# A mixture-of-experts stage behind a gated recurrence: from all experts on all tokens to tokens sorted by expert, gathered and scattered by indirect DMA

## The chip, the cores and the metric

One Trainium2 chip, one of its cores, one launch. Times are device microseconds of that core; a result is the median of its runs. The engines are TensorE (PE, its weight loads as PEld), VectorE (DVE), ScalarE (ACT), GpSimd (POOL) and SyncE (SP, which here only issues DMAs).

## What is computed

The kernel has two parts. The first is a gated linear recurrence in 768 steps for 4 batches of 8 heads of width 48, with a complex decay: `S = a * S + k v^T`, `y_t = q_t S_re`. Its output, put side by side by heads, is a matrix x of 3072 tokens by 384. The second part is a mixture of experts on x. For each token, 8 logits are x times a gate matrix plus a bias that the token's modality picks; the largest logit picks the expert, and its softmax probability is the weight of the result:

```python
logits = x @ w_gate + modality_bias[modality_id]
e_idx = np.argmax(logits, axis=1)
for e in range(E):
    mask = e_idx == e
    h = np.maximum(x[mask] @ w1[e], 0.0)
    out[mask] = gate_w[mask, None] * (h @ w2[e])
```

w1 is 8 x 384 x 1024 and w2 is 8 x 1024 x 384, in float32. Only one expert of eight is needed for a token.

## The kernel before

The kernel is written in a tile framework: tiles come from pools with a number of buffers, and the framework puts in the semaphores. It orders each engine's instructions by program order and by when they can start, so an engine's queue may differ from the text: a tile whose space is taken from closed pools waits for the tiles that held it.

**Attention, 6 chunks of 128 steps.** For each of 32 (batch, head) pairs a helper, `load_t` (L159 to L166), loads a 128x48 piece through SP into `raw` (two buffers), transposes it on PE and copies it on VectorE; it runs for a_re, a_im, q and k. VectorE then normalises the decay and forms its running products over the chunk in seven doubling steps (L194 to L211). A loop over the 32 heads (L242 to L282) multiplies on PE with VectorE copies between; `y_sb` (L261, two buffers) holds a head's 128x48 result, which PE transposes, VectorE copies to `yT_sb` (L265), and SP stores to `x_attn` in HBM with tokens along the row (L267). Sixteen VectorE instructions (L288 to L303) then carry the state to the next chunk. `gstack.close()` gives the space of these tiles back.

**Experts, `moe_bf16` (L18).** x is loaded transposed, as one 4.7 MB DMA (L32), and cast to bf16 (L34). For 24 tiles of 128 tokens, three f32 matmuls with an 8-wide moving side make the logits (L47), and small VectorE and ScalarE instructions make a table `sc_all` that has the gate weight in the column of the picked expert and zero elsewhere (L71). Then every expert runs on every token: for each expert its float32 weights are loaded through SP (L81, L85) and cast on VectorE (L82, L86), two buffers each; for each of 6 blocks of 512 tokens and each of 8 slices of F there are three matmuls 512 wide (L93), a relu on VectorE from PSUM to bf16 (L95), and four matmuls 384 wide that sum into four PSUM banks (L97). At the block's end VectorE multiplies by the table's column and adds to `out_acc` (L100). The last expert's results are stored tile by tile (L102). The lines after the early `return` in the main function never run.

Of the kernel before, what the change touches and what calls it, by code (L numbers as in the profile page):

```python
# [17 lines left out]
def moe_bf16(nc, ctx, tc, cpool, ppool, x_dram, moe_modality_id, moe_w_gate, moe_modality_bias, moe_w1, moe_w2, out):  # L18
    Dt, N = x_dram.shape
# [3 lines left out]
    nDC = Dt // 128  # L23
    nT = 128
    nTiles = N // nT
    nF = F // 128

    mp = ctx.enter_context(tc.tile_pool(name="mp", bufs=2))
    mbig = ctx.enter_context(tc.tile_pool(name="mbig", bufs=1))

    xT = mbig.tile([128, nDC, N], F32, name="xT")
    nc.sync.dma_start(out=xT[:], in_=x_dram.rearrange("(dc p) n -> p dc n", p=128))  # L32
    xTb = mbig.tile([128, nDC, N], BF16, name="xTb")
    nc.vector.tensor_copy(xTb[:], xT[:])  # L34

    mb_raw = cpool.tile([1, nM * E], F32, name="mb_raw")
# [367 lines left out]
```

## Time and profile before

| | us |
|---|---|
| median of 3 runs | 4122.12 |
| lowest and highest run | 4119.45 and 4122.41 |
| span of the profiled execution, first to last instruction | 4111.5 |
| median less span | 10.6 |
| attention stage, to its last state update | 3525.4 |
| load of x, gate, experts | 586.1 |

The time of the profiled execution is known by its span alone; it is set against the median of the runs. In the rows below, PE and PEld are two rows of one engine, "x" is a count, a releaser is what an engine waited for last, and "SPq" is the queue of DMA issues on SP. Matmul ends are modelled, so the start-to-start distance of matmuls tells more than their duration.

### The profile page before, as it was taken

The page shows a single profiled execution, that of the slowest core. Times are in us where ns is not written, and L with a number is a line of the kernel's source. Part 1 is how long each engine was busy: PE and PEld are TensorE (multiplying, and loading weights), DVE is VectorE, ACT ScalarE, POOL GpSimd, SP SyncE. Part 2 cuts the span into 40 slices and gives each one's busy share as a digit, 9 for nine tenths or more (in the row PEclk, how much of TensorE's full clock was granted, in tenths as well). Part 3 has the DMA queues.
Part 4 walks back from the last instruction along what each step waited for, and adds up shares of the span by engine and source line. Part 5 has one row for each costly group of instructions (what it writes and reads, how often), then busy time and mean ns, then how long its engine had stood idle before and what let it go on. Part 6 is the DMA issues. An engine that isn't in the chain of part 4 may idle for free.

```text
span 4111.5 us, 21704 instructions
## 1 busy us (share of the span) xinstructions
PE 1639.4 (40%) x6816; PEld 959.5 (23%) x6864; DVE 2761.7 (67%) x3610; ACT 29.2 (1%) x32; POOL 57.5 (1%) x199
## 2 busy tenths in 40 slices
PE   2002751013740015720027610137400157599999
PEld 0000540002520004500005400025200035444444
DVE  4997246986248984259972469872489842877676
ACT  0000000000000000000000000000000000000000
POOL 0000000000000000000000000000000000000000
PEclk9999999999999999999999999999999999999999
DMA  1000000000010000010000000000100000401001
GB/s 25 0 2 13 5 16 11 0 9 8 5 22 5 0 12 6 5 25 0 0 15 5 15 13 0 7 9 5 21 6 0 12 5 5 170 31 62 31 1 47
DMA packets 167188, 64.41 MB, mean 16 GB/s; under 512 B 143138, under 2 KB 163618, under 8 KB 166690
## 3 DMA queue, kind: packets, MB, share of 16 engines
q1 hardware_dynamic: 167074, 63.02, 6.1%
q8 instruction: 56, 0.92, 0.1%
q14 instruction: 58, 0.48, 0.0%
HBM read 53.51 MB, written 9.44 MB: 15 GB/s over the span
## 4 chain that ended last, share of the span: by engine, by line
DVE 51%; PE 33%; DMA 10%; issue 3%; POOL 1%; ACT 1%; DVEq 0%; POOLq 0%; SPq 0%; ACTq 0%
PE z_ps L97 6%; PE hT_ps L93 5%; DVE qc L203 4%; DVE kc L204 4%; DVE kc L201 4%; DVE qc L200 4%; DVE cr L185 4%; DVE qc L231 4%; DMA raw<-in_a_im_dram 3%; PE Wt_ps L252 3%; DMA raw<-in_q_dram 3%; PE y_ps L258 3%; PE tp L165 3%; PE y_ps L259 3%; DMA raw<-in_a_re_dram 3%
## 5 line engine op out<-in xcount | busy, mean ns | idle before, releaser
L165 PE MATMUL tp<-ident,raw 128*48 128x128 f32 x768 | 286.6, 384 | 2052.1 <-DVE qc L166 1315.0
L165 PEld LDWEIGHTS tp<-ident,raw 128*48 128x48 f32 x768 | 88.3, 116 | 2249.1 <-DVE qc L166 1432.1
L95 DVE TENSOR_SCALAR hT<-hT_ps 128x512 bf16<-128x512 f32 x384 | 254.2, 689 | 134.4 <-PE hT_ps L93 119.3
L262 DVE COPY y_sb<-y_ps 128x48 f32<-128x48 f32 x192 | 39.9, 208 | 409.5 <-PE y_ps L260 409.5
L97 PE MATMUL z_ps<-w2e,hT 128*128 128x384 bf16 x1536 | 283.8, 328 | 9.0 <-DVE hT L95 7.0
L93 PE MATMUL hT_ps<-xTb,w1e 128*128 128x512 bf16 x1104 | 271.2, 380 | 2.8 <-issue 0.2
L252 PE MATMUL Wt_ps<-are,cr 48*128 48x128 f32 x384 | 152.3, 499 | 107.0 <-DVE cr L235 107.0
L258 PE MATMUL y_ps<-vc,Wt 128*128 128x48 f32 x384 | 127.0, 431 | 161.8 <-POOL Wt L256 161.8
L255 DVE COPY Wt<-Wt_ps 128x128 f32<-128x128 f32 x192 | 55.9, 291 | 190.5 <-PE Wt_ps L253 190.5
L97 PEld LDWEIGHTS <-hT 128*128 128x128 bf16 x1536 | 122.3, 97 | 177.7 <-DVE hT L95 127.1
L185 DVE RECIPROCAL cr<-cr 48x4096 f32<-48x4096 f32 x6 | 154.5, 25745 | 0.2
L231 DVE RECIPROCAL qc<-qc 48x4096 f32<-48x4096 f32 x6 | 154.4, 25734 | 0.0
L258 PEld LDWEIGHTS y_ps<-vc,Wt 128*128 128x128 f32 x384 | 96.2, 311 | 218.3 <-POOL Wt L256 218.3
L166 DVE COPY aim<-tp 48x128 f32<-48x128 f32 x192 | 52.5, 282 | 133.5 <-PE tp L165 133.3
L93 PEld LDWEIGHTS <-w1e 128*128 128x128 bf16 x1152 | 113.1, 98 | 118.5 <-issue 1.3
L166 DVE COPY are<-tp 48x128 f32<-48x128 f32 x192 | 52.3, 281 | 115.0 <-PE tp L165 114.5
L259 PE MATMUL y_ps<-S0rA,are 48*128 48x48 f32 x384 | 126.7, 428 | 0.0
L252 PEld LDWEIGHTS Wt_ps<-are,cr 48*128 48x128 f32 x384 | 95.9, 308 | 125.6 <-DVE cr L235 108.7
L253 PE MATMUL Wt_ps<-aim,ci 48*128 48x128 f32 x384 | 121.1, 417 | 0.0
L260 PE MATMUL y_ps<-S0iA,kc 48*128 48x48 f32 x384 | 119.7, 410 | 0.0
L266 DVE COPY yT_sb<-yT_ps 48x128 f32<-48x128 f32 x192 | 54.3, 283 | 96.4 <-PE yT_ps L264 96.4
L166 DVE COPY qc<-tp 48x128 f32<-48x128 f32 x192 | 50.1, 280 | 101.7 <-PE tp L165 101.4
(101 smaller groups left out, 2984.6 us busy)
## 6 DMA issues: line engine op xcount, KB each, us to landing
w1f<-in_moe_w_dram SPq DMA_DIRECT2D x8, 1536.0 KB, 6.5
w2f<-in_moe_w_dram SPq DMA_DIRECT2D x8, 1536.0 KB, 8.2
vc<-in_v_dram SPq DMA_DIRECT2D x24, 192.0 KB, 3.7
raw<-in_a_re_dram SPq DMA_DIRECT2D x192, 24.0 KB, 1.7
raw<-in_a_im_dram SPq DMA_DIRECT2D x192, 24.0 KB, 1.6
raw<-in_q_dram SPq DMA_DIRECT2D x192, 24.0 KB, 1.7
raw<-in_k_dram SPq DMA_DIRECT2D x192, 24.0 KB, 1.7
x_attn<-yT_sb SPq DMA_DIRECT2D x192, 24.0 KB, 1.4
```

The source lines that it names most:

```text
L93: nc.tensor.matmul(hT_ps[:], w1e[:, dc, fc * 128:(fc + 1) * 128], xTb[:, dc, t0:t0 + TTK], start=(dc == 0), stop=(dc == nDC - 1))
L95: nc.vector.tensor_relu(hT[:], hT_ps[:])
L97: nc.tensor.matmul(z_ps[z][:], hT[:, z * nT:(z + 1) * nT], w2e[:, fc, :], start=(fc == 0), stop=(fc == nF - 1))
L165: nc.tensor.transpose(tp[:], raw[:], ident[:L, :L])
L185: nc.vector.reciprocal(tmp[:], tmp[:])
L200: nc.vector.tensor_tensor(tA[:, :, :, :n_], a_hi, a_lo, Alu.mult)
L201: nc.vector.tensor_tensor(tB[:, :, :, :n_], b_hi, b_lo, Alu.mult)
L203: nc.vector.tensor_tensor(tA[:, :, :, :n_], a_hi, b_lo, Alu.mult)
L231: nc.vector.reciprocal(qf[:], qf[:])
L252: nc.tensor.matmul(Wt_ps[:], Kr[:], Qr[:], start=True, stop=False)
L258: nc.tensor.matmul(y_ps[:], Wt[:], vb, start=True, stop=False)
L259: nc.tensor.matmul(y_ps[:], Qr[:], S0r[bh][:], start=False, stop=False)
```

## The change

The expert stage is written anew as `moe_sorted`. Attention also stores `y_sb`, with tokens as rows, to a second HBM tensor `x_rows`. All 8 experts' weights are loaded once through POOL's queue by DMAs that cast to bf16, into two tiles that hold all experts. Logits are computed with the gate as the stationary side and transposed back. Each token gets a slot number from its expert: matmuls with triangular and all-one matrices count tokens before it, and scans make the experts' offsets, each rounded up to 128. One-hot products of slot and token invert the permutation into `idg` (a token for each slot), `ids` (the same, with 8192 or so, out of bounds, for an empty slot) and the gate weight of each slot. Then 31 slots of 128 tokens run: an indirect DMA gathers the slot's rows of x with a cast to bf16, the slot's expert number is loaded into a PE register, PE transposes the rows, multiplies with that expert's weights by a register-addressed slice, VectorE and ScalarE share the relu, ScalarE scales, and an indirect DMA scatters the rows to the output, leaving out-of-bounds rows out. The main function's dead code goes, and the attention stage's PSUM pool is closed with it.

Core of the diff:

```diff
@@ moe_bf16 -> moe_sorted @@
-def moe_bf16(nc, ctx, tc, cpool, ppool, x_dram, moe_modality_id, moe_w_gate, moe_modality_bias, moe_w1, moe_w2, out):
...
-    for nt in range(nTiles):
-        n0 = nt * nT
-        lg_ps = ppool.tile([nT, E], F32, name="lg_ps", tag="r", bufs=4)
-        for dc in range(nDC):
-            nc.tensor.matmul(lg_ps[:], xT[:, dc, n0:n0 + nT], wg[:, dc, :], start=(dc == 0), stop=(dc == nDC - 1))
...
-        w1e = mp.tile([128, nDC, F], BF16, name="w1e")
-        w1f = mp.tile([128, nDC, F], F32, name="w1f")
-        nc.sync.dma_start(out=w1f[:], in_=moe_w1[e].rearrange("(dc p) f -> p dc f", p=128))
-        nc.vector.tensor_copy(w1e[:], w1f[:])
-        w2e = mp.tile([128, nF, Dt], BF16, name="w2e")
-        w2f = mp.tile([128, nF, Dt], F32, name="w2f")
-        nc.sync.dma_start(out=w2f[:], in_=moe_w2[e].rearrange("(fc p) d -> p fc d", p=128))
-        nc.vector.tensor_copy(w2e[:], w2f[:])
-        for tk in range(nTK):
-            t0 = tk * TTK
-            z_ps = [ppool.tile([nT, Dt], F32, name=f"z_ps{i}", tag=f"z{i}", bufs=1) for i in range(TTK // nT)]
-            for fc in range(nF):
-                hT_ps = ppool.tile([128, TTK], F32, name="hT_ps", tag="r", bufs=4)
-                for dc in range(nDC):
-                    nc.tensor.matmul(hT_ps[:], w1e[:, dc, fc * 128:(fc + 1) * 128], xTb[:, dc, t0:t0 + TTK], start=(dc == 0), stop=(dc == nDC - 1))
-                hT = mp.tile([128, TTK], BF16, name="hT")
-                nc.vector.tensor_relu(hT[:], hT_ps[:])
-                for z in range(TTK // nT):
-                    nc.tensor.matmul(z_ps[z][:], hT[:, z * nT:(z + 1) * nT], w2e[:, fc, :], start=(fc == 0), stop=(fc == nF - 1))
-            for z in range(TTK // nT):
-                nt = tk * (TTK // nT) + z
-                nc.vector.scalar_tensor_tensor(out_acc[:, nt, :], z_ps[z][:], sc_all[:, nt, e:e + 1], out_acc[:, nt, :], Alu.mult, Alu.add)
-    for nt in range(nTiles):
-        nc.sync.dma_start(out=out[nt * nT:(nt + 1) * nT, :], in_=out_acc[:, nt, :])
+def moe_sorted(nc, ctx, tc, cpool, ident, x_t_dram, x_rows_dram, moe_modality_id, moe_w_gate, moe_modality_bias, moe_w1, moe_w2, out):
...
+    mp = ctx.enter_context(tc.tile_pool(name="mp", bufs=1))
+    fp = ctx.enter_context(tc.tile_pool(name="fp", bufs=3))
+    pp = ctx.enter_context(tc.psum_pool(name="pp", bufs=1))
+    w1s = mp.tile([128, E, KD, F], BF16, name="w1s")
+    w2s = mp.tile([128, E, NF, Dt], BF16, name="w2s")
+    xT = mp.tile([128, KD, N], F32, name="xT", tag="xT")
+    wg = mp.tile([128, KD, E], F32, name="wg")
+    mb = mp.tile([128, nM, E], F32, name="mb")
+    mid = mp.tile([128, NT, 2], I32, name="mid")
+    nc.sync.dma_start(out=wg[:], in_=moe_w_gate.rearrange("(k p) e -> p k e", p=128))
+    nc.sync.dma_start(out=mb.rearrange("p m e -> p (m e)"), in_=moe_modality_bias.rearrange("m e -> (m e)")[None, :].broadcast_to([128, nM * E]))
+    nc.sync.dma_start(out=mid[:], in_=moe_modality_id.bitcast(I32).rearrange("(t p two) -> p t two", p=128, two=2))
+    for k in range(KD):
+        nc.sync.dma_start(out=xT[:, k, :], in_=x_t_dram[k * 128:(k + 1) * 128, :])
     for e in range(E):
+        nc.gpsimd.dma_start(out=w1s[:, e], in_=moe_w1[e].rearrange("(k p) f -> p k f", p=128))
+        nc.gpsimd.dma_start(out=w2s[:, e], in_=moe_w2[e].rearrange("(c p) d -> p c d", p=128))
...
+    io128 = mp.tile([128, 128], F32, name="io128")
+    nc.gpsimd.iota(io128[:], pattern=[[1, 128]], base=0, channel_multiplier=0, allow_small_or_imprecise_dtypes=True)
+    idp1 = mp.tile([128, NT], F32, name="idp1")
+    nc.gpsimd.iota(idp1[:], pattern=[[128, NT]], base=1, channel_multiplier=1, allow_small_or_imprecise_dtypes=True)
+    pref = mp.tile([128, E], F32, name="pref")
+    nc.gpsimd.iota(pref[:], pattern=[[-1, E]], base=E, channel_multiplier=0, allow_small_or_imprecise_dtypes=True)
...
+    lg_ps = pp.tile([128, NT, E], F32, name="lg_ps")
+    for j in range(N // 512):
+        ps = pp.tile([E, 512], F32, name="lgT_ps", tag="r", bufs=2)
+        lgT = fp.tile([E, 512], F32, name="lgT", bufs=2)
+        sl = slice(j * 512, (j + 1) * 512)
+        for k in range(KD):
+            nc.tensor.matmul(ps[:], wg[:, k, :], xT[:, k, sl], start=(k == 0), stop=(k == KD - 1))
+        nc.scalar.copy(lgT[:], ps[:])
+        for i in range(4):
+            nc.tensor.transpose(lg_ps[:, 4 * j + i, :], lgT[:, i * 128:(i + 1) * 128], ident[:E, :E])
...
+    cand = mp.tile([128, NT, E], F32, name="cand")
+    nc.vector.scalar_tensor_tensor(cand[:], sh[:], 0.0, pref[:, None, :].broadcast_to([128, NT, E]), Alu.is_ge, Alu.mult)
+    best = mp.tile([128, NT], F32, name="best")
+    nc.vector.tensor_reduce(best[:], cand[:], axis=AX.X, op=Alu.max)
+    oneh = mp.tile([128, NT, E], BF16, name="oneh")
+    nc.vector.tensor_tensor(oneh[:], cand[:], bc(best, E), Alu.is_equal)
+    rank_ps = pp.tile([128, NT, E], F32, name="rank_ps", tag="rk")
+    nc.tensor.matmul(rank_ps.rearrange("p t e -> p (t e)"), trib[:], oneh.rearrange("p t e -> p (t e)"), start=True, stop=True)
+    cnt_ps = pp.tile([128, NT, E], F32, name="cnt_ps", tag="ct")
+    nc.tensor.matmul(cnt_ps.rearrange("p t e -> p (t e)"), onesb[:], oneh.rearrange("p t e -> p (t e)"), start=True, stop=True)
+    cnt = mp.tile([128, E, NT], F32, name="cnt")
+    nc.vector.tensor_copy(cnt[:], cnt_ps.rearrange("p t e -> p e t"))
+    inc = mp.tile([128, E, NT], F32, name="inc")
+    nc.vector.tensor_tensor_scan(inc.rearrange("p e t -> p (e t)"), seg0.rearrange("p e t -> p (e t)"), cnt.rearrange("p e t -> p (e t)"), 0.0, Alu.mult, Alu.add)
...
+    texp = mp.tile([128, H32], I32, name="texp")
+    nc.vector.tensor_scalar(texp[:], texp_f[:], float(E - 1), None, Alu.min)
...
+    onlo = mp.tile([128, NT, 128], F32, name="onlo", tag="xT")
+    nc.vector.tensor_tensor(onlo[:], io128[:, None, :].broadcast_to([128, NT, 128]), bc(lo, 128), Alu.is_equal)
...
+    inv_ps = pp.tile([128, 2, H32], F32, name="inv_ps", tag="ct")
+    for t in range(NT):
+        nc.tensor.matmul(inv_ps.rearrange("p a h -> p (a h)"), onlo[:, t, :], load[:, t].rearrange("p a h -> p (a h)"), start=(t == 0), stop=(t == NT - 1))
...
+    idg = mp.tile([128, H32], U32, name="idg")
+    nc.vector.tensor_scalar(idg[:], inv[:, 0, :], -1.0, 0.0, Alu.add, Alu.max)
+    empty = mp.tile([128, H32], F32, name="empty")
+    nc.vector.tensor_scalar(empty[:], inv[:, 0, :], 0.0, 8192.0, Alu.is_equal, Alu.mult)
+    ids = mp.tile([128, H32], U32, name="ids")
+    nc.vector.scalar_tensor_tensor(ids[:], inv[:, 0, :], -1.0, empty[:], Alu.add, Alu.add)
+    for i in range(NS):
+        xg = fp.tile([128, Dt], BF16, name="xg", bufs=4)
+        nc.gpsimd.indirect_dma_start(out=xg[:], out_offset=None, in_=x_rows_dram, in_offset=bass.IndirectOffsetOnAxis(ap=idg[:, i:i + 1], axis=0))
+        te = nc.values_load(texp[0:1, i:i + 1], engines=[ET.PE], min_val=0, max_val=E - 1, skip_runtime_bounds_check_because="a count of at most E, cut at E - 1")
+        xg_ps = pp.tile([128, KD, 128], BF16, name="xg_ps", tag="rk")
+        for k in range(KD):
+            nc.tensor.transpose(xg_ps[:, k, :], xg[:, k * 128:(k + 1) * 128], identb[:])
+        xgT = fp.tile([128, KD, 128], BF16, name="xgT")
+        nc.vector.tensor_copy(xgT[:], xg_ps[:])
+        hT = fp.tile([128, NF, 128], BF16, name="hT", bufs=2)
+        for g in range(2):
+            h_ps = pp.tile([128, NF // 2, 128], F32, name="h_ps", tag="r", bufs=2)
+            for f in range(NF // 2):
+                ff = g * (NF // 2) + f
+                for k in range(KD):
+                    nc.tensor.matmul(h_ps[:, f, :], w1s[:, bass.ds(te, 1), k, ff * 128:(ff + 1) * 128], xgT[:, k, :], start=(k == 0), stop=(k == KD - 1))
+            gs = slice(g * (NF // 2), (g + 1) * (NF // 2))
+            if g == 0:
+                nc.vector.tensor_relu(hT[:, gs], h_ps[:])
+            else:
+                nc.scalar.activation(hT[:, gs], h_ps[:], Act.Relu)
+        y_ps = pp.tile([128, Dt], F32, name="y_ps", tag="y", bufs=2)
+        for f in range(NF):
+            nc.tensor.matmul(y_ps[:], hT[:, f, :], w2s[:, bass.ds(te, 1), f, :], start=(f == 0), stop=(f == NF - 1))
+        y_sb = fp.tile([128, Dt], F32, name="y_sb")
+        nc.scalar.activation(y_sb[:], y_ps[:], Act.Copy, scale=inv[:, 1, i:i + 1])
+        nc.gpsimd.indirect_dma_start(out=out, out_offset=bass.IndirectOffsetOnAxis(ap=ids[:, i:i + 1], axis=0), in_=y_sb[:], in_offset=None, bounds_check=N - 1, oob_is_err=False)
...
     x_dram = nc.dram_tensor("x_attn", (Dt, N), F32, kind="Internal").ap()
+    x_rows = nc.dram_tensor("x_rows", (N, Dt), F32, kind="Internal").ap()
 
     cpool = ctx.enter_context(tc.tile_pool(name="c", bufs=1))
-    ppool = ctx.enter_context(tc.psum_pool(name="ps", bufs=2))
     gstack = ExitStack()
+    ppool = gstack.enter_context(tc.psum_pool(name="ps", bufs=2))
...
             y_sb = pool.tile([L, D], F32, name="y_sb")
             nc.vector.tensor_copy(y_sb[:], y_ps[:])
+            nc.sync.dma_start(out=x_rows[b * S + t0:b * S + t0 + L, h * D:(h + 1) * D], in_=y_sb[:])
             yT_ps = ppool.tile([D, L], F32, name="yT_ps", tag="r", bufs=4)
             nc.tensor.transpose(yT_ps[:], y_sb[:], ident[:L, :L])
             yT_sb = pool.tile([D, L], F32, name="yT_sb")
...
     gstack.close()
-    if True:
-        moe_bf16(nc, ctx, tc, cpool, ppool, x_dram, moe_modality_id, moe_w_gate, moe_modality_bias, moe_w1, moe_w2, out)
-        return
...
+    moe_sorted(nc, ctx, tc, cpool, ident, x_dram, x_rows, moe_modality_id, moe_w_gate, moe_modality_bias, moe_w1, moe_w2, out)
```

## Rows read from the trace of the kernel before

**Rows 1.** Page, part 1: busy us, share of the span, instructions, by engine

```profile
PE 1639.4 (40%) x6816; PEld 959.5 (23%) x6864; DVE 2761.7 (67%) x3610; ACT 29.2 (1%) x32; POOL 57.5 (1%) x199
```

**Rows 2.** Windows by stage: length, busy us of each engine, granted clock, DMA share, GB/s

```profile
0.00:3504.45 3504.45, 1087.80 (x4032) 693.24 (x4032) 2316.68 (x2716) 22.98 (x7) 57.47 (x199) 1.00 0.04 8
3504.45:3525.40 20.95, 0.00 (x0) 0.00 (x0) 20.95 (x25) 0.00 (x0) 0.00 (x0) 1.00 0.82 280
3525.40:3540.74 15.34, 0.00 (x0) 0.00 (x0) 13.44 (x8) 0.00 (x0) 0.00 (x0) 1.00 0.99 374
3540.74:3588.26 47.52, 44.21 (x201) 36.81 (x203) 42.17 (x287) 6.18 (x25) 0.00 (x0) 1.00 0.36 122
3588.26:4111.50 523.24, 507.41 (x2584) 229.47 (x2629) 368.49 (x580) 0.00 (x0) 0.00 (x0) 1.00 0.10 34
```

**Rows 3.** Chain that ended last, expert stage: start us, us, what

```profile
3588.26 2.32 PE hT_ps L93 x10
...
3599.12 2.32 PE hT_ps L93 x10
```

**Rows 4.** Groups, 3588.26 to 4111.50: xcount | busy, mean ns | idle before, releaser

```profile
L97 PE MATMUL z_ps<-w2e,hT 128*128 128x384 bf16 x1504 | 277.1, 327 | 8.7 <-DVE hT L95 7.0
...
L95 DVE TENSOR_SCALAR hT<-hT_ps 128x512 bf16<-128x512 f32 x376 | 248.7, 689 | 134.0 <-PE hT_ps L93 118.9 <-PE z_ps L97 15.1
...
L93 PEld LDWEIGHTS <-w1e 128*128 128x128 bf16 x1125 | 110.1, 98 | 115.3
...
L100 DVE SCALAR_TENSOR_TENSOR out_acc<-z_ps,sc_all,out_acc 128x384 f32<-128x384 f32 x192 | 105.2, 611 | 18.2 <-PE z_ps L97 18.2
```

**Rows 5.** Timeline, expert stage: start us, us, engine, line, what

```profile
3590.61 1.47 PE L97 MATMUL z_ps<-w2e,hT 128*128 128x384 bf16 x8
```

**Rows 6.** Timeline, attention: the same step of two heads, and a store on SP

```profile
3434.68 0.66 PE L258 MATMUL y_ps<-vc,Wt 128*128 128x48 f32 x2 [0.81 <-POOL Wt L256]
...
3440.16 0.66 PE L258 MATMUL y_ps<-vc,Wt 128*128 128x48 f32 x2 [0.82 <-POOL Wt L256]
...
3503.53 0.30 SPq L267 DMA_DIRECT2D x_attn<-yT_sb  x1
```

**Rows 7.** Timeline, between the stages: loads on SP and the last state update

```profile
3505.26 0.42 SPq L81 DMA_DIRECT2D w1f<-in_moe_w_dram  x1
...
3523.66 1.74 DVE L303 TENSOR_TENSOR S0iA<-tB,tD 48x1536 f32<-48x1536 f32 x1
...
3525.48 0.38 SPq L32 DMA_DIRECT2D xT<-x_attn  x1
```

**Rows 8.** DMA issues: queue, op xcount, KB each, median us to landing

```profile
raw<-in_a_re_dram SPq DMA_DIRECT2D x192, 24.0 KB, 1.7
...
x_attn<-yT_sb SPq DMA_DIRECT2D x192, 24.0 KB, 1.4
...
xT<-x_attn SPq DMA_DIRECT2D x1, 4608.0 KB, 14.7
...
out_dram<-out_acc SPq DMA_DIRECT2D x24, 192.0 KB, 1.9
```

**Rows 9.** Groups of the whole span: prices of small instructions

```profile
L256 POOL TENSOR_SCALAR_AFFINE_SELECT Wt<-Wt 128x128 f32<-128x128 f32 x192 | 56.5, 294 | 3429.8 <-DVE Wt L255 3429.8
...
L47 PE MATMUL lg_ps<-wg,xT 128*128 128x8 f32 x144 | 31.7, 362 | 39.1 <-DMA mid_raw<-in_moe_modality_id_dram 36.5 <-DVE logits L49 2.4
...
L180 DVE TENSOR_TENSOR ci<-aim 48x4096 f32<-48x4096 f32 x6 | 26.5, 4417 | 0.2
...
L61 DVE TENSOR_REDUCE mx<-logits 128x1 f32<-128x8 f32 x24 | 3.6, 152 | 0.0
```

**Rows 10.** Timeline, first matmuls of the expert stage

```profile
3576.04 1.91 PE L93 MATMUL hT_ps<-xTb,w1e 128*128 128x512 bf16 x4 [0.22 <-issue]
...
3576.04 0.15 PEld L93 LDWEIGHTS <-w1e 128*128 128x128 bf16 x1 [0.28 <-issue]
...
3578.78 0.81 PE L93 MATMUL hT_ps<-xTb,w1e 128*128 128x512 bf16 x3
```

More of the change, by code (lines that the diff above doesn't have):

```diff
@@ L22, in moe_bf16 @@
     nM = moe_modality_bias.shape[0]
[L23 to L36, printed above, removed]
@@ new lines, in moe_sorted, with bc @@
+    nc.vector.memset(one8[:], 1.0)
+    zero8 = mp.tile([128, E], F32, name="zero8")
+    nc.vector.memset(zero8[:], 0.0)
+    onesb = mp.tile([128, 128], BF16, name="onesb")
+    nc.vector.memset(onesb[:], 1.0)
+    trib = mp.tile([128, 128], BF16, name="trib")
+    nc.vector.tensor_copy(trib[:], onesb[:])
+    nc.gpsimd.affine_select(trib[:], trib[:], pattern=[[1, 128]], compare_op=Alu.is_gt, fill=0.0, base=0, channel_multiplier=-1)
+    def bc(ap, n):
+        return ap[:, :, None].broadcast_to([128, NT, n])
@@ new lines, in moe_sorted @@
+    bias = mp.tile([128, NT, E], F32, name="bias")
+    is_m = mp.tile([128, NT], F32, name="is_m", tag="is_m", bufs=2)
+    nc.vector.tensor_scalar(is_m[:], mid[:, :, 0], 0.0, None, Alu.is_equal)
+    nc.vector.tensor_tensor(bias[:], bc(is_m, E), mb[:, 0:1, :].broadcast_to([128, NT, E]), Alu.mult)
+    for m in range(1, nM):
+        is_m = mp.tile([128, NT], F32, name="is_m", tag="is_m", bufs=2)
+        nc.vector.tensor_scalar(is_m[:], mid[:, :, 0], float(m), None, Alu.is_equal)
+        bias_m = mp.tile([128, NT, E], F32, name="bias_m")
+        nc.vector.tensor_tensor(bias_m[:], bc(is_m, E), mb[:, m:m + 1, :].broadcast_to([128, NT, E]), Alu.mult)
+        nc.vector.tensor_tensor(bias[:], bias[:], bias_m[:], Alu.add)
@@ new lines, in moe_sorted @@
+    thr = mp.tile([128, NT], F32, name="thr")
+    nc.gpsimd.iota(thr[:], pattern=[[128, NT]], base=0, channel_multiplier=0, allow_small_or_imprecise_dtypes=True)
+    nc.vector.tensor_tensor(need[:], inc[:, :, NT - 1:NT].broadcast_to([128, E, NT]), thr[:, None, :].broadcast_to([128, E, NT]), Alu.is_gt)
+    tiles = mp.tile([128, E], F32, name="tiles")
+    nc.vector.tensor_reduce(tiles[:], need[:], axis=AX.X, op=Alu.add)
+    ends = mp.tile([128, E], F32, name="ends")
+    nc.vector.tensor_tensor_scan(ends[:], one8[:], tiles[:], 0.0, Alu.mult, Alu.add)
@@ new lines, in moe_sorted @@
+    past = mp.tile([128, H32, E], F32, name="past")
+    nc.vector.tensor_tensor(past[:], ends[:, None, :].broadcast_to([128, H32, E]), io128[:, 0:H32, None].broadcast_to([128, H32, E]), Alu.is_le)
+    texp_f = mp.tile([128, H32], F32, name="texp_f")
+    nc.vector.tensor_reduce(texp_f[:], past[:], axis=AX.X, op=Alu.add)
+    texp = mp.tile([128, H32], I32, name="texp")
+    nc.vector.tensor_scalar(texp[:], texp_f[:], float(E - 1), None, Alu.min)
+    beg = mp.tile([128, E], F32, name="beg")
+    nc.vector.tensor_tensor(beg[:], ends[:], tiles[:], Alu.subtract)
@@ new lines, in moe_sorted @@
+    off = mp.tile([128, E, NT], F32, name="off")
+    nc.vector.scalar_tensor_tensor(off[:], beg[:, :, None].broadcast_to([128, E, NT]), 128.0, inc[:], Alu.mult, Alu.add)
+    nc.vector.tensor_tensor(off[:], off[:], cnt[:], Alu.subtract)
+    slot = mp.tile([128, NT, E], F32, name="slot")
+    nc.vector.tensor_tensor(slot[:], off.rearrange("p e t -> p t e"), rank_ps[:], Alu.add)
+    nc.vector.tensor_tensor(slot[:], slot[:], oneh[:], Alu.mult)
+    pos = mp.tile([128, NT], F32, name="pos")
+    nc.vector.tensor_reduce(pos[:], slot[:], axis=AX.X, op=Alu.add)
@@ new lines, in moe_sorted @@
+    pos_i = mp.tile([128, NT], I32, name="pos_i")
+    nc.vector.tensor_copy(pos_i[:], pos[:])
+    lo_i = mp.tile([128, NT], I32, name="lo_i")
+    nc.vector.tensor_scalar(lo_i[:], pos_i[:], 127, None, Alu.bitwise_and)
+    lo = mp.tile([128, NT], F32, name="lo")
+    nc.vector.tensor_copy(lo[:], lo_i[:])
+    hi_i = mp.tile([128, NT], I32, name="hi_i")
+    nc.vector.tensor_scalar(hi_i[:], pos_i[:], 7, None, Alu.logical_shift_right)
+    hi = mp.tile([128, NT], F32, name="hi")
+    nc.vector.tensor_copy(hi[:], hi_i[:])
@@ new lines, in moe_sorted @@
+    sm = mp.tile([128, NT], F32, name="sm")
+    nc.vector.tensor_reduce(sm[:], ex[:], axis=AX.X, op=Alu.add)
+    gw = mp.tile([128, NT], F32, name="gw")
+    nc.vector.reciprocal(gw[:], sm[:])
+    onlo = mp.tile([128, NT, 128], F32, name="onlo", tag="xT")
+    nc.vector.tensor_tensor(onlo[:], io128[:, None, :].broadcast_to([128, NT, 128]), bc(lo, 128), Alu.is_equal)
+    onhi = mp.tile([128, NT, H32], F32, name="onhi")
+    nc.vector.tensor_tensor(onhi[:], io128[:, None, 0:H32].broadcast_to([128, NT, H32]), bc(hi, H32), Alu.is_equal)
@@ new lines, in moe_sorted @@
+    load = mp.tile([128, NT, 2, H32], F32, name="load")
+    nc.vector.tensor_tensor(load[:, :, 0, :], onhi[:], bc(idp1, H32), Alu.mult)
+    nc.vector.tensor_tensor(load[:, :, 1, :], onhi[:], bc(gw, H32), Alu.mult)
+    inv_ps = pp.tile([128, 2, H32], F32, name="inv_ps", tag="ct")
+    for t in range(NT):
+        nc.tensor.matmul(inv_ps.rearrange("p a h -> p (a h)"), onlo[:, t, :], load[:, t].rearrange("p a h -> p (a h)"), start=(t == 0), stop=(t == NT - 1))
+    inv = mp.tile([128, 2, H32], F32, name="inv")
```

121 lines of the change are left out of this document (25 added, 96 removed).

## Prediction

> **What bounds the kernel now.** I read the page's busy shares first, then busy time by stage, then the groups of instructions of the last stage, the timeline of its steps, the hand-over between the two stages, and the list of DMAs. The page says that no engine is full: VectorE (DVE) is busy 67% of the span, TensorE (PE) 40% [rows 1]. That average hides two kernels in a row. By stage [rows 2], the attention recurrence runs to 3504.5 us and its last state update to 3525.4; there PE is busy 31% and waits on VectorE and on DMAs. The change leaves all that arithmetic alone. Then 15.3 us load x, 47.5 us compute the gate, and from 3588.3 to the end, 523.2 us, PE is busy 507.4: PE bounds the expert stage. It repeats every 10.86 us [rows 3], one such group for each of 8 experts and 6 blocks of 512 tokens, 48 x 10.87 = 522. Within it eight 384-wide matmuls take 1.47 us, 0.184 each [rows 5], and VectorE's relu (689 ns) and weighted sum (611 ns) lie beside them [rows 4]. So what is to be won is at most the 586 us from 3525.4 to 4111.5.
>
> **The change, part by part.** (1) *The extra store of y in the attention stage.* 192 stores of 24 KB go into SP's queue, each ahead of the store of yT that is there already. A store holds SP for 0.30 us, a head takes 5.48 us (start to start) [rows 6], and such a store lands in 1.4 us [rows 8]. y_sb has two buffers, so the next writer of a buffer comes 10.96 us later. Cost 0, hidden under the head; with that cover gone it would be 192 x 0.30 = 58 us. What stands behind it on SP is the store of yT (0.3 us later at most) and, once in a chunk, the loads of the next chunk, which wait for buffers anyway. Nothing is gained either.
>
> (2) *Weights: sixteen loads with a cast, on POOL's queue, in place of sixteen on SP.* Their space is that of attention tiles which come free with the last head; the old kernel's first weight load shows when, 3505.3 [rows 7]. 16 x 1536 KB are 25.2 MB, and x adds 4.7 MB: 29.9 MB. In the x load's stretch the queues moved 374 GB/s at a DMA share of 0.99 [rows 2], so all of it takes at least 80 us: not before 3585. Before, these loads spread over the expert stage and cost nothing; now every slot picks its expert by register, so the first matmul waits for all sixteen. A cast during a transfer is not in this trace. It could cost nothing (the bytes read are the same) or, if building or casting halves the rate, 160 us: 3665. The sixteen VectorE casts, which lay beside PE's work, go away.
>
> (3) *The x load* still waits for the last state update and is issued at 3525.5 [rows 7]. Alone it landed in 14.7 us [rows 8]; now it shares engines that are full with weights, so I double it: 3555.
>
> (4) *Logits and routing.* Eighteen f32 matmuls 512 wide replace 72 that were 8 wide. Bounds: two passes at the bf16 pace of 0.21 (see (5)) give 8 us, four times that 31; I take 16, since an f32 matmul shows two records and such a pass costs more than a bf16 one (0.22 us for 8 columns, 144 records in 31.7 us [rows 9]). Logits stand at 3571. The chain after them has some 31 small VectorE instructions of 128x192 or less: 0.15 us and 192 columns at 1.08 ns (4417 ns for 4096) make 0.35 each [rows 9], 11 us; one 3072 wide, 3.3; three 768 wide, 2.7; 24 f32 matmuls with 128x128 weights and a narrow moving side, two records each at 0.22, 10.4; hops between engines 2.6. Together 30 us. POOL's iotas (pref, io128) feed this chain and stand behind the weight loads on POOL. If POOL issues at SP's pace it is free early, and the chain ends at 3601; if it can build descriptors only as fast as data moves, it is free at about 3584 and the chain ends at 3614. First gather 4 us (an issue and a landing of 1.7 [rows 8], rounded up for the unseen indirect kind). I start the slots at **3615**, near the later of the two, because the same moment also frees the weights. Bounds: 3586 and 3669.
>
> (5) *31 slots of 128 tokens* replace 48 groups. 31 x 128 is 3968 token places where there were 24576. With the reference's draw only two experts get tokens, 1526 and 1546, so 25 slots are filled; the other six run all the same. A slot has 3 transposes, 24 matmuls 128 wide with a weight load each, and 8 that are 384 wide. At the expert stage's pace: 24 x 0.098 (a weight load, longer than 128 columns of streaming) [rows 4] + 8 x 0.184 [rows 5] + 3 x 0.18 = 4.4 us. But the same engine has a slower pace in this trace: the first four expert matmuls, behind 8-wide ones, took 1.91 us, while three a little later took 0.81 [rows 10]. With the last one's latency taken off, that is what 512 columns need at the two clock levels, 0.43 us at 1.2 GHz and 0.21 at 2.4, though the granted clock of the stretch reads 1.00 [rows 2]. At the slow pace a slot costs 24 x 0.15 (that stretch's weight load) + 8 x 0.32 + 0.6 = 6.8 us. The Trainium skill, TensorE: Matmul & The Clock Gate, "HAM oscillation", says that matmuls in bursts with waits between them fall back to the low clock. By that rule the slots stay at 6.8 us; by the clock column alone they would be 4.4. I take **6.8**, since a slot is short, thin and broken by hand-overs, as the work ahead of those four matmuls was. Register loads and address arithmetic on PE's sequencer are unseen: at least nothing, at most as much again as the issue of 32 more instructions at the densest pace seen (0.098), 3.1 us in a slot. The Trainium skill, DMA: Bandwidth & Descriptors, "Latency and other measured facts", gives a floor of about 600 ns for a tensor load; by it, if nothing hides the load, 31 x 0.6 = 19 us would be added. VectorE's copy and relu (about 0.6 + 0.69) and ScalarE's two instructions lie under PE. POOL's two indirect DMAs too, up to 3.4 us each; the nearest rows are a POOL instruction of 0.29 us [rows 9] and an SP issue of 0.30 [rows 6].
>
> (6) *Tail:* ScalarE's copy, the scatter's issue and its landing, 6 us (a store before lands in about 2).
>
> **Sum:** 3615 + 31 x 6.8 = 211, + 6 = 3832 us of span. The profiled span, 4111.5, lies 10.6 under the median of the runs; with the same outside, **3843 us**, 279 (6.8%) less than before.
>
> **Rivals.** *A. The array at its full pace,* 4.4 us a slot: 3615 + 136 + 16.6 = 3768. For it: every clock reading is 1.00. Against: rows 10 show how thin work leaves the engine, and address work comes on top.
>
> *B. The slot becomes a chain.* If a gather waits behind the scatter of the slot before it in POOL's one queue, nothing overlaps: gather 2.0, transposes 0.7, copy 0.6, first product 3.6, relu 0.7, second 2.6, copy 0.6, scatter 0.3: 11.1 us a slot and 3615 + 344 + 16.6 = 3976. A sequencer that spends that long on register addresses gives the same number. For it: one POOL queue, one buffer for the transposed tile in PSUM. Against: four gather buffers, and the framework fills gaps (in the old trace too).
>
> *C. The weights come late,* at half the rate: slots start at 3669, end at 3886, 3897 in all. For: the cast and 11264 pieces built in software. Against: bytes and engines are the same as in rows 2 and 8.
>
> *D. Slower than before: POOL's indirect DMAs bound the slots.* Between 3615 and 4105 there are 490 us, 15.8 a slot, two indirect DMAs each: from 7.9 us of POOL time for one on, the kernel loses. At 9 it would be 3615 + 558 + 16.6 = 4190. For: software must build 256 pieces for each, and no row shows it. Against: 7.9 is 26 times the nearest rows.
>
> *E. The work saved is not saved.* The slots could still run 8 experts; the diff says no: one expert's columns in each slot, so no time of its own.
>
> **How the numbers follow.** Chances: forecast 0.52, A 0.14, B 0.17, C 0.12, D 0.05. All but D are faster by over 0.2% (8 us, about what a measurement of this kernel can tell from no change); a landing within 8 us of before would be D at its exact break-even, 0.01. So faster 0.95, same 0.01, slower 0.04. The range runs from the earliest start with A's slots, 3586 + 136 + 16.6 = 3739, to B's 3976: 3740 to 3980. It leaves out D and the far part of B.
>
> **What would show it.** Right: the attention stage still ends near 3525 and heads keep 5.48 us; the x load lands near 3555; weights land by 3600; the first slot matmul comes near 3615; slots repeat every 6.8 us with PE busy, matmuls 384 wide at 0.32. Wrong: slots at 4.4 with 0.184 (A), PE waiting on a gather or an "issue" gap that repeats once a slot (B), PE waiting on a weight DMA with the ids long ready (C), POOL busy from end to end (D), or a head longer than 5.48 us (the store in (1)).

## The result, and the profile after

The changed kernel takes **3890.89 us** (median of 4 runs, 3889.84 to 3893.69) against 4120.78 for the kernel before in the same session: a ratio of **0.9445, 95% interval 0.9431 to 0.9458**. That is 230 us less where 279 were forecast; the time lies inside the range and 48 us above the point. The profiled execution took 3889.84 us, with a span of 3888.1.

Busy time by stage, the view that answers to [rows 2] (columns: length, busy us of PE, PEld, DVE, ACT and POOL with their counts, granted clock, DMA share, GB/s):

```profile
0.00:3506.90 3506.90, 1086.89 (x4032) 693.69 (x4032) 2315.76 (x2715) 22.98 (x7) 56.79 (x198) 1.00 0.05 10
...
3527.80:3550.80 23.00, 0.00 (x0) 0.01 (x1) 2.10 (x13) 0.00 (x0) 9.18 (x11) 1.00 1.08 207
3550.80:3574.40 23.60, 20.24 (x60) 4.60 (x60) 0.00 (x0) 3.92 (x7) 3.27 (x4) 1.00 1.17 264
3574.40:3606.80 32.40, 10.96 (x51) 10.52 (x51) 14.90 (x35) 1.17 (x2) 5.03 (x10) 0.56 1.20 203
...
3700.00:3800.00 100.00, 93.39 (x399) 44.43 (x399) 11.99 (x23) 13.04 (x23) 21.98 (x22) 0.62 0.15 34
```

The stages are attention, its last state updates (left out), x's transfer, logits, sorting and first gather, and a hundred microseconds of slots. Attention is nearly as long as it was (to 3527.8 against 3525.4); what follows it lasts 360 us in place of 586. In the slots PE is busy 93% of the time, against 97% in the old expert stage, but the granted clock, 1.00 there, reads 0.62.

The hand-over, in the timeline (columns: start, us, engine, line, what, and in brackets the idle time before it with its releaser):

```profile
3528.65 0.95 POOL L52 DMA_DIRECT2D w1s<-in_moe_w_dram  x1 [25.35 <-DVE onesb L72]
...
3574.41 0.36 DVE L105 TENSOR_TENSOR lg<-lg_ps,bias 128x192 f32<-128x192 f32 x1 [27.20 <-PE lg_ps L103]
...
3576.20 0.90 POOL L53 DMA_DIRECT2D w2s<-in_moe_w_dram  x1 [3.12 <-DMA w2s<-in_moe_w_dram]
3577.10 0.26 POOL L59 IOTA io<- 128x128 f32 x1
...
3602.55 1.03 POOL L195 DMA_INDIRECT xg<-x_rows,idg  x1 [24.65 <-DVE empty L189]
...
3606.79 0.50 PE L199 MATMUL xg_ps<-identb,xg 128*128 128x128 bf16 x3 [5.01 <-DMA xg<-x_rows,idg]
...
3608.36 5.58 PE L208 MATMUL h_ps<-xgT,w1s 128*128 128x128 bf16 x24 [1.07 <-DMA xg<-x_rows,idg]
```

Weights are issued from 3528.65 to 3576.20 (the DMA share falls from 1.25 to 0.73 in the window from 3606 to 3610, so they end at about 3608), logits stand at 3574.4, sorting ends at 3602.4, the first gather takes 4.24 us from issue to the first transpose. From there to the end of the last slot's second layer, 3882.44, are 31 slots: 275.6 us, **8.89 us each** where 6.8 were forecast.

One slot of the steady state (same columns):

```profile
3705.07 0.36 DVE L201 COPY xgT<-xg_ps 128x384 bf16<-128x384 bf16 x1 [4.61 <-PE xg_ps L199]
...
3705.48 5.67 PE L208 MATMUL h_ps<-xgT,w1s 128*128 128x128 bf16 x24 [0.45 <-DVE xgT L201]
...
3708.69 1.69 PEld L208 LDWEIGHTS <-w1s 128*128 x8 [0.20 <-issue]
...
3710.94 0.42 PE L199 MATMUL xg_ps<-identb,xg 128*128 128x128 bf16 x2
...
3711.15 2.76 PE L216 MATMUL y_ps<-w2s,hT 128*128 x8
...
3713.71 0.31 PE L199 MATMUL xg_ps<-identb,xg 128*128 128x128 bf16 x1
...
3714.47 4.63 PE L208 MATMUL h_ps<-xgT,w1s 128*128 128x128 bf16 x20 [0.45 <-DVE xgT L201]
...
3715.52 1.68 PEld L208 LDWEIGHTS <-w1s 128*128 x8 [0.16 <-issue]
```

By starts, a slot of 8.99 us is 5.46 for the first layer, 0.21 for two transposes of the next slot, 2.56 for the second layer (0.32 a matmul), 0.31 for the third transpose and 0.45 of waiting for its copy. The second layer is as forecast; the first takes 5.46 where 3.6 were. It runs at the same pace at either clock: eight weight loads take 1.69 us from 3708.69 on, where all half-microsecond windows show the granted clock at its low level (1.2 GHz), and 1.68 from 3715.52 on, where all show it at its high one (2.4 GHz). One window of each:

```profile
3709.50:3710.00 0.50, 0.50 (x4) 0.21 (x2) 0.00 (x0) 0.00 (x0) 0.00 (x0) 0.50 0.00 0
...
3716.00:3716.50 0.50, 0.48 (x3) 0.24 (x3) 0.00 (x0) 0.00 (x0) 0.50 (x1) 1.00 0.65 69
```

So the clock does not set this pace. The view of line L208 over that one slot (columns: engine, operation, count, shortest/median/longest ns, first and last start; PEldq is the queue of the loads) shows what stands between the loads, and that of L216 the same for the second layer:

```profile
L208 PEldq FUSED_REGOPS  x48: 51/55/60, 3705.5 to 3713.0; - x48
...
L208 PEld LDWEIGHTS <-w1s x24: 95/105/147, 3705.6 to 3713.7; 128*128 x24
```

```profile
L216 PEldq FUSED_REGOPS  x8: 51/55/55, 3710.9 to 3712.3; - x8
```

There are two register operations of 55 ns for each of the 24 matmuls of the first layer, where the operand picked by register is the one that is loaded, and one for each of the 8 of the second, where it is the streamed one: in the first layer 105 + 2 x 55 = 215 ns, against 1.69 / 8 = 211 measured. The rest of the 5.46 us are gaps of 0.15 to 0.20 after every eighth load.

### The profile page after: what moved, and what is told of

It is laid out like the page before. It is cut to its first block, busy times and chain, and to the rows that moved or that the text cites. A ratio compares the mean times of both kernels' runs of the same rounds, so it can differ in the third digit from the quotient of the medians.

```text
span 3888.1 us, 19678 instructions
## 1 busy us (share of the span) xinstructions
PE 1374.7 (35%) x5227; PEld 830.2 (21%) x5227; DVE 2385.9 (61%) x2837; ACT 64.6 (2%) x77; POOL 132.5 (3%) x281
## 5 line engine op out<-in xcount | busy, mean ns | idle before, releaser
L208 PE MATMUL h_ps<-xgT,w1s 128*128 128x128 bf16 x744 | 169.4, 250 | 19.0 <-DVE xgT L201 13.4
L374 POOL TENSOR_SCALAR_AFFINE_SELECT Wt<-Wt 128x128 f32<-128x128 f32 x192 | 56.1, 292 | 3445.8 <-DVE Wt L373 3445.8
L378 PEld LDWEIGHTS y_ps<-S0iA,kc 48*128 48x128 f32 x384 | 104.3, 330 | 0.0
L371 PEld LDWEIGHTS Wt_ps<-aim,ci 48*128 48x128 f32 x384 | 104.3, 330 | 0.0
L201 DVE COPY xgT<-xg_ps 128x384 bf16<-128x384 bf16 x31 | 11.1, 357 | 150.3 <-PE xg_ps L199 150.3
```

Of the source, the lines that this page charges most:

```text
L208: nc.tensor.matmul(h_ps[:, f, :], w1s[:, bass.ds(te, 1), k, ff * 128:(ff + 1) * 128], xgT[:, k, :], start=(k == 0), stop=(k == KD - 1))
L371: nc.tensor.matmul(Wt_ps[:], Ki[:], Qi[:], start=False, stop=True)
L374: nc.gpsimd.affine_select(Wt[:], Wt[:], pattern=[[1, L]], compare_op=Alu.is_ge, fill=0.0, base=0, channel_multiplier=-1)
L378: nc.tensor.matmul(y_ps[:], negQi[:], S0i[bh][:], start=False, stop=True)
```

## Experiments

Two theories stood at the start. **R:** register arithmetic in PE's load queue sets the pace. **K:** the low clock sets it. The kernel before was run beside each of these; the chips differ by up to 0.3%, so ratios are compared, with 0.9445 as the changed kernel's.

**Constants for the experts.**

```diff
-te = nc.values_load(texp[0:1, i:i + 1], engines=[ET.PE], ...)
+es = 2 if i < 12 else 4 if i < 25 else 7
-... w1s[:, bass.ds(te, 1), k, ...]      w2s[:, bass.ds(te, 1), f, :]
+... w1s[:, es, k, ...]                  w2s[:, es, f, :]
```

> The expert of each slot is written into the program as a constant (2 for slots 0 to 11, 4 for 12 to 24, 7 after them, which is what this draw gives), so the register load and all register-made addresses go; the arithmetic is the same. Theory R (register arithmetic in PE's load queue): in the changed kernel the 24 first-layer matmuls of a slot stand 0.21 us apart at the high and at the low granted clock alike, which is a load of 105 ns and two register operations of 55 ns; without them the pitch falls to the load's 0.105 to 0.12 us, the slot from 8.90 to 5.7 to 6.2 us, and the time by 31 x 2.7 to 3.2 us, to 3791 to 3807 us. Theory K (clock): the granted clock of 0.62 in the slots sets the pitch, a load of 105 ns and a pass of 107 ns one after the other; then the pitch stays 0.21 us, the slot 8.6 to 8.9 us, and the time 3881 to 3891 us.

Measured: 3751.02 us, ratio 0.9076 [0.9062, 0.909], which is 0.0369 x 4121 = 152 us less than the changed kernel, 4.9 us a slot. K falls, and R's 2.7 to 3.2 us a slot are not the whole gain. The first slot and a later one of this run in the timeline:

```profile
3621.47 2.72 PE L208 MATMUL h_ps<-xgT,w1s 128*128 128x128 bf16 x24 [0.45 <-DVE xgT L201]
...
3623.98 0.42 PE L199 MATMUL xg_ps<-identb,xg 128*128 128x128 bf16 x2
...
3688.94 1.50 PE L208 MATMUL h_ps<-xgT,w1s 128*128 128x128 bf16 x24 [0.45 <-DVE xgT L201]
```

Busy time and clock around the first layer of the first slot, over the whole of that slot and over the rest:

```profile
3619.00:3623.00 4.00, 2.03 (x18) 1.87 (x19) 0.41 (x2) 0.00 (x0) 2.66 (x3) 0.50 0.68 80
...
3620.50:3626.10 5.60, 5.13 (x38) 4.10 (x39) 1.05 (x2) 0.61 (x2) 1.47 (x2) 0.60 0.46 53
3627.00:3743.00 116.00, 97.34 (x1042) 67.20 (x1039) 31.11 (x59) 34.74 (x59) 55.15 (x56) 1.00 0.31 64
```

The first layer of the first slot runs at the low clock and takes 2.51 us by starts for the 24 matmuls, 0.105 each; so at the *same* clock the register operations cost 0.211 - 0.105 = 0.106 us a matmul, 2.5 us a slot, and 5.46 - 2.51 = 2.95 with the gaps after every eighth load, which this run does not have: R's number. But without them the clock reads 1.00 from 3627 on: the first layer takes 1.5 us, the second 1.47 to 1.7, the slot 3.96 on average. The other 2 us a slot are the clock, which the register operations had held down. In the changed kernel's half-microsecond windows from 3700 to 3720 it falls within the first layer of both slots and rises about when the second layer has ended. That they held it down is shown, not how: PE waits 0.45 us for the copied tile in both kernels, and in the faster one that wait is a larger share of the slot. Whether loads spaced out by something else than register operations would hold it down too was not tried.

**Constants for the second layer alone.** Edit: as above, only `w2s[:, es, f, :]`.

> Only the second layer's weights get the constant expert; the first layer keeps the register. Theory R: the 8 register operations of the second layer lie under passes of 0.32 us each, so the slot keeps its 8.9 us and the time is 3886 to 3892 us. A variant of R, in which every register operation costs its 55 ns wherever it stands, gives 31 x 8 x 0.055 = 14 us, 3877 us. Theory K: no change.

Measured: 3906.99 us against 4133.9, ratio 0.9452 [0.9437, 0.9466], no change. A register operation costs nothing where a pass of 384 columns covers it; the price is not one per operation but one per operation that stands in line with short loads.

**Half a dose.** Constants for half of the first layer, and for the second layer too.

```diff
-w1s[:, bass.ds(te, 1), k, ...]
+(w1s[:, es, k, ...] if g == 0 else w1s[:, bass.ds(te, 1), k, ...])
```

> Constants for half of the first layer (the 12 matmuls of the first group) and for the second layer; the other 12 first-layer matmuls keep the register. By the runs so far a first-layer matmul costs 0.211 us with register addresses at either clock level, 0.107 without them at the low level and 0.06 at the high one. If a dose of 12 already holds the clock at the low level: slot 8.90 - 12 x 0.104 = 7.65 us, 39 us less than the changed kernel, a ratio to the kernel before of about 0.935. If the clock stays high and only the issue is paid: 12 x 0.211 + 12 x 0.06 + 1.46 + 1.0 = 5.7 us, 99 us less, about 0.9205.

Measured: ratio 0.9296 [0.928, 0.9311], 61 us less than the changed kernel, 2.0 a slot: between the two cases. The windows say why: the clock does neither of the two things expected but lies between (0.81 and 0.75, against 0.62 and 1.00):

```profile
3625.00:3700.00 75.00, 67.81 (x414) 37.47 (x413) 11.89 (x23) 14.13 (x24) 22.87 (x23) 0.81 0.20 44
3700.00:3800.00 100.00, 91.24 (x510) 49.48 (x510) 15.37 (x29) 17.08 (x29) 29.00 (x29) 0.75 0.20 41
```

Within a slot it is high while the twelve constant matmuls run and low by the second layer. More register operations, more time at the low clock.

**Work added to lift the clock.**

```diff
+for _ in range(4):
+    nc.tensor.matmul(fill_ps[:], identb[:], w1s[:, 0, 0, 0:512], start=True, stop=True)
```

> The changed kernel, register addresses and all, with four added matmuls of 512 columns at fixed addresses in each slot, where PE waits for the copy of the gathered tile; their result is not used. They take 0.85 us at the high clock or 1.7 us at the low one, of which 0.8 us fits into the wait. Theory R with the clock as a second, separate cost: the clock rises, the first layer keeps its 0.21 us a matmul, the second layer falls from 2.5 to 1.4 us: slot about 7.5 us, 42 us less, ratio about 0.934. If the clock is the cause of the 0.21 us: the first layer falls too, slot about 5 us, 120 us less, 0.915. If they don't lift the clock: slot 9.8 us, 28 us more, 0.951.

Measured: 3908.57 us, ratio 0.9459 [0.9443, 0.9475], 6 us more and inside the intervals of no change; none of the three cases. The clock rose only part of the way, to 0.70 in the window from 3700 to 3800, which paid for about what the fillers cost. As a test of K it still answers: in the timeline a run of eight first-layer loads lies wholly in a stretch of high clock, and it takes the same 1.68 us.

```profile
3710.34 1.68 PEld L211 LDWEIGHTS <-w1s 128*128 x8 [0.28 <-issue]
```

The half-microsecond windows over it:

```profile
3710.50:3711.00 0.50, 0.48 (x3) 0.19 (x2) 0.00 (x0) 0.00 (x0) 0.12 (x1) 1.00 0.94 138
...
3711.50:3712.00 0.50, 0.48 (x3) 0.24 (x3) 0.50 (x1) 0.00 (x0) 0.00 (x0) 1.00 0.31 111
```

**The register used once a slot for the first layer, on DVE.** The second layer keeps its register on PE, so the kernel stays general.

```diff
+w1c = fp.tile([128, KD, F], BF16, name="w1c", bufs=2)
+nc.vector.tensor_copy(w1c[:, None, :, :], w1s[:, bass.ds(te, 1)])
-... w1s[:, bass.ds(te, 1), k, ...]
+... w1c[:, k, ...]
```

> The register picks the first layer's weights once a slot, on DVE, which copies the expert's 128 x 3072 bf16 into one of two small tiles a slot ahead; PE reads that tile at a fixed address. Theory R: as with constants, 3791 to 3810 us, as long as DVE's copy (not measured yet; at the pace of its 128 x 384 copy of 0.36 us it would be 2.9 us) fits beside its 1.05 us of other work in a slot of about 6 us. Theory K: no gain, 3885 to 3895 us. A third way, in which DVE's copy stands ahead of the next copy or relu that PE waits for, gives 31 x up to 2 us back of R's gain, 3810 to 3870 us.

Measured: 3767.14 us, ratio 0.9115 [0.9101, 0.9129], 136 us less. The group of the copies (columns as in [rows 4]):

```profile
L196 DVE COPY w1c<-w1s 128x3072 bf16 x31 | 29.8, 961 | 21.4 <-DMA w1s<-in_moe_w_dram 18.9 <-PE h_ps L215 2.2 <-issue 0.2
```

A copy takes 0.96 us, not 2.9. The gain stays 16 us under that of the constants, because the first copy reads by register, so waits for all sixteen loads, and stands in DVE's queue in the middle of the sorting: 18.9 us of idle DVE. (The first transposes come 19.7 us later after the last state update than with constants; the slots are then 0.1 us shorter.) A wait moved from PE, where it cost 0.6 us, to an engine with a chain behind it.

**No store of y rows in attention.** Edit: the `dma_start` of L381 taken out, and the gather's source replaced.

> The second store of y in attention (x_rows) is left out, and the gather reads rows of moe_w2 in its place, so the output is not the layer's. The prediction put this store at nothing. If so: 3888 to 3893 us, no change. If the 2.4 us by which attention ended later than before is the store's wait for its place in SP's queue: 2 to 3 us less, about 3888 us. A store that holds every head a little, 192 x 0.05 us, would give 10 us, 3881 us.

Measured: 3906.82 us against 4133.9, ratio 0.9452 [0.9439, 0.9465]. No change: the store is free, as predicted. The later end of attention is not its doing: without it the last state update ends at 3544.0, and at 3541.3 to 3543.1 in the three runs above on the same chip, a scatter as wide as the 2.4 us in question.

**Weights after x.**

```diff
+nc.gpsimd.tensor_tensor(w1s[:, :, 0, 0], xT[:, 0, 0:E], xT[:, 1, 0:E], Alu.add)
+nc.gpsimd.tensor_tensor(w2s[:, :, 0, 0], xT[:, 1, 0:E], xT[:, 2, 0:E], Alu.add)
 (the sixteen weight loads, moved behind these and behind the iotas)
```

> The weight loads wait until xT has landed, and the iotas stand ahead of them on POOL. If the chain of logits and sorting bounds the start of the slots, and the weights only slowed xT's load: xT lands 8 to 10 us earlier and so do the slots, ratio about 0.9425 against 0.9445 of the changed kernel. If the weights' own transfer bounds it as well (the first register-addressed matmul of the changed kernel, which waits for every expert, began at 3608.36 right as the transfers ended): the logits move up and the first slot still begins at 3608 to 3612 with PE waiting for weights, 0 to 4 us more, 0.9445 to 0.9455.

Measured: ratio 0.9448 [0.9433, 0.9464], no change, though the sorting was done 15.5 us sooner: the first gather is issued 59.2 us after the last state update's end (3540.55 in this run), against 74.7 in the changed kernel. Timeline, the gather and the first transposes:

```profile
3599.75 1.02 POOL L197 DMA_INDIRECT xg<-x_rows,idg  x1 [9.20 <-DVE empty L191]
...
3620.22 0.50 PE L201 MATMUL xg_ps<-identb,xg 128*128 128x128 bf16 x3 [21.23 <-DMA xg<-x_rows,idg]
```

The gathers, which used to land in 3.5 us, now take 18.8 (median of seven): they are issued while the weights still fill the DMA engines, and land when these are through. The transfers bound the start as well as the sorting does; with the sorting alone made earlier, nothing is gained.

**Weights cast ahead, in DRAM.**

```diff
+nc.gpsimd.dma_start(out=w1b[e], in_=moe_w1[e])     (and w2b; in the scan of chunk 1; w1b, w2b bf16 in DRAM)
-nc.gpsimd.dma_start(out=w1s[:, e], in_=moe_w1[e]...)
+nc.sync.dma_start(out=w1s[:, e], in_=w1b[e]...)
```

> The weights are cast to bf16 once, from DRAM to DRAM, while attention's scan of the second chunk keeps the DMA engines idle, and are then loaded as bf16 (half the bytes, on SP behind xT). If transfers are what the start of the slots waits for: xT lands at about 3542, the logits are done by 3560, the weights are in by 3576, the slots begin at about 3590 in place of 3607: 15 to 18 us less, ratio about 0.9405. If the sorting's chain does not follow xT: no change, 0.9445. If the casts delay attention's own loads: up to 20 us more, 0.949.

Measured: 3888.66 us against 4131.94, ratio 0.9413 [0.9397, 0.9429], 13 us less. The first transposes come 62.2 us after the last state update's end (3603.02 after 3540.81), against 79.0, so the start gained 16.8 us. Some 3.6 of it are lost at the end: from the end of the last scatter's issue to the end of the span are 7.4 us (3879.6 to 3887.0) in place of 3.8 (3884.3 to 3888.1). Both runs below, which also cast ahead, have the same 7.4; no row shows what fills them.

**The parts put together.** Edit: the two above, the next slot's transposes and copy between the two layers with two PSUM tiles for them, and the first copy held behind the sorting by reading the experts from a tile that is computed last.

> A version made of the parts that paid: the weights cast ahead in DRAM and loaded as bf16 (13 us in its own run), the first layer's weights copied once a slot by DVE (0.96 us a copy in its own run; 136 us, of which some 19 us were lost to a first copy that waited for the weights in the middle of the sorting), that first copy held behind the sorting's end, and the transposes and copy of the next slot's tokens put between the two layers of a slot with a second PSUM tile, which takes the 0.8 us wait for the copied tile out of each slot. By theory R: slot 3.7 less 0.5 to 0.8, about 3.1 us, 31 x 3.1 = 96 us, slots starting 13 to 16 us earlier than the changed kernel's: 3890 - 276 + 96 - 13 = about 3697 us on that chip, a ratio of 0.893 to 0.903. If POOL becomes the bound (two indirect DMAs of 1.0 us and 0.3 us behind each, with scatters that waited for each other's landing in the copy run): slots stay at 3.7 us and the ratio is 0.903 to 0.908. If the clock falls back to the low level: slot 5 us, 0.913.

Measured: 3731.05 us against 4130.45, ratio **0.9032 [0.9017, 0.9047]**; it keeps the register, so it serves any draw. That is 170 us less than the changed kernel, on the border of the first two cases expected. The clock reads 1.00 from 3640 to 3700, so the third did not come; but the slots stay at about 3.4 us, not 3.1. What they wait for now (columns: waiter, releaser, us, times, longest):

```profile
POOL out_dram L243 <- ACT y_sb L242: 36.4, 22, 4.2
...
ACT y_sb L242 <- DMA out_dram<-y_sb,ids: 30.6, 12, 4.1
```

Three buffers hold the scaled output, and each is free only when its scatter has landed. Eight buffers:

> The version before, with eight buffers in place of three for the scaled output tile, whose scatter to DRAM frees it. In that version ACT stood 30.6 us in 12 waits for a scatter to land, with PE at 1.5 us a first layer and 3.4 us a slot, and scatters stand 2.86 us apart at the least, each issued after the one before has landed. If the buffers are the limit: ACT's waits go and the slot falls to 3.1 us, 8 to 12 us less, ratio 0.900 to 0.9015. If the chain of scatters is the limit (0.97 us of issue and 1.9 us of landing each, with a gather between): the waits move from ACT to POOL, and the time stays within 3 us, 0.9025 to 0.904.

Measured: ratio 0.9042 [0.9027, 0.9057], the same, so the buffers are not the limit. ACT's waits for a landing are gone; POOL now waits, and its last scatters stand 2.85 us apart with nothing else in its queue:

```profile
3707.96 0.97 POOL L243 DMA_INDIRECT out_dram<-y_sb,ids  x1 [1.89 <-ACT y_sb L242]
3710.81 0.97 POOL L243 DMA_INDIRECT out_dram<-y_sb,ids  x1 [1.88 <-issue]
3713.68 0.97 POOL L243 DMA_INDIRECT out_dram<-y_sb,ids  x1 [1.89 <-DMA out_dram<-y_sb,ids]
```

0.97 us of issue and 1.9 of waiting. The profile puts the 1.9 down to ScalarE, to nothing and to the scatter before in turn; it is the even spacing that speaks for a scatter that goes out only when its predecessor has landed. With a gather between them, scatters of this run stand 3.37 us apart (3675.07, 3678.44, 3681.80), which is the slot. This is argued, not shown: the chain itself was not taken away, since all scatters write one output by indices. Without it POOL would still hold some 2.6 us of a slot, an estimate from the same rows: two issues of 1.00 and 0.30 behind each.

## Why the prediction was right, and where it was off

The forecast case held: PE bounds the slots, at the low clock. Against the terms of the sum:

| step | forecast | measured |
|---|---|---|
| (2) weights | from 3505.3, 80 us of transfer | from 3528.65 to about 3608, 79 us |
| (4) logits done | 3571 | 3574.4 |
| (4) sorting's end | 3601 or 3614 | 3602.4 |
| (4) slots start | 3615 | 3606.8 |
| (5) a slot | 6.8 | 8.89 |
| (6) last slot to the end of the span, and outside it | 6 + 10.6 | 5.7 + 1.7 |

The start is 8.2 us early, the slots 31 x 2.09 = 64.8 us long, the end 9.2 us short: +47.4, against 3889.84 - 3843 = +46.8. So the time came nearer to the point than its largest term did, by two errors, 17 us together, in the other direction. Most of the end's 9.2 was never time outside the span: in each timed run of the kernel before that stands beside an experiment, the span is 1.7 us less than the time, as in the changed kernel. The 10.6 us set the span of one execution against the median of others, which were some 9 us slower.

**(5), the mis-sized term,** is the first layer's 24 x 0.15 with the register work beside it. The text bounded register work at 0 to 3.1 us a slot and took nothing. The direct cost is 2.5 us, 2.95 with the gaps. Taking it at the bottom of its range was the error: the trace of before had no row that says the issue is covered, and a 128-wide matmul of 0.105 us covers almost none of it. The rest of the term, 0.15 a matmul for the low clock, was 0.045 too dear, and the third transpose with the wait for its copy 0.76 in place of part of 0.6.

**The clock** was judged right by [rows 10], for the second layer exactly (0.32). But the reason was wrong, and the right level was luck: the prediction let the clock follow from short slots with hand-overs and saw register work as an addition at one clock. The runs show them coupled: without the register operations the same short slots with the same hand-overs hold 1.00, and rival A, 4.4 us a slot, is about what the constants gave (3.96). By the Trainium skill, TensorE: Matmul & The Clock Gate, "HAM oscillation", waits between bursts bring the low clock; the outcome agrees here (0.62), but the constants' run has the same 0.45 us wait in each slot and reads 1.00, so such waits are not what held this clock down. The Trainium skill's floor of about 600 ns for a tensor load (DMA: Bandwidth & Descriptors, "Latency and other measured facts") does not show in this trace: the load of a slot's expert number took 304 ns, and it lies under the second layer:

```profile
L196 PEldq TENSOR_LOAD <-texp x1: 304/304/304, 3712.5 to 3712.5; - x1
```

**(1)** was right: heads still take 5.48 us, and the run without the store shows no gain. **(2)** had the rate right and the moment wrong: POOL's first load waited 25.35 us and went out 0.8 us after the last state update, not with the last head. It cost 0.6 us, the excess of the first product's wait of 1.07 us over the usual 0.45, since the sorting was as late. **(3)** fits: x's parts landed 20.8 us (median) after an issue from 3529.5 on, and the logits began at 3550.8. **(4)** the iotas did stand behind the weight loads, to 3577.1; DVE waited 0.91 us for them.

**Rivals.** B did not come: POOL waits for PE, and an indirect DMA takes it 0.97 us (gather) or 1.02 (scatter) to issue, so D's break-even of 7.9 us was far off. B named the right place, a sequencer with register addresses, with a price of 11.1 us a slot that was too high. C's half rate did not come, though the weights were within a microsecond of being the bound. A chain of POOL's scatters, not of gather behind scatter as in B, seems to be there at 2.9 us a scatter, hidden under slots of 8.9.

## What to carry to other kernels

Pick a weight by register where the instruction behind it is long: once a slot on an idle engine (0.96 us a copy here, 136 us saved), or as the wide streamed operand, where it cost nothing; as the loaded operand of 128-wide matmuls it cost two operations of 55 ns each time and the high clock besides. An operation that no row shows and that stands in the queue of the bound engine is not to be taken at the bottom of its range; here it cost 2.95 of the 3.1 us. Where two waits end within a microsecond of each other, remove both before judging either.

## What was not expected of the hardware

- The granted clock followed how the matmuls were issued: 0.62 with 24 register-addressed first-layer matmuls in a slot, 0.75 to 0.81 with 12, 1.00 with none, at PE busy shares of 93%, 91% and 84%. PE's busy share does not order these runs: with the fillers it was 96% and the clock 0.70.
- In the stretch of the logits the clock column reads 1.00; in the sorting, with PE idle but for two small matmuls, it falls (0.54 from 3578 to 3582, 0.50 after it), and the 48 records of L183 (10.47 us) and the first slot run at the low level, with constants too.
- Gathers issued while 25 MB of weights were under way landed in 18.8 us (median) instead of 3.5.
